# Two pads of 352 bytes per partition that move the feed-forward's later weight parts and the experts' second weights in on-chip memory

## The chip, the cores and the metric

The program runs on one core of a Trainium2 chip. The metric is the device time of one execution in microseconds (us). Before the change it is 1409.03 us, the median of three runs (1408.67, 1409.03 and 1420.4).

## What is computed

An attention with pooled keys and values, then a layer of eight experts of which each token uses at most one, then a dense feed-forward. The last part, cut to its core, is

```python
def _moe2_ref(x, w_in, w_out):       # x [4608, 512], w_in [512, 2048], w_out [2048, 512]
    h = x @ w_in
    g = h * (1.0 / (1.0 + np.exp(-h)))
    return (g @ w_out).astype(np.float32)
```

and inside the expert layer each expert computes `np.maximum(xc @ w1[e], 0.0) @ w2[e]`, with `w1[e]` of 512 x 1024 and `w2[e]` of 1024 x 512. Everything is float32 to the outside, and the feed-forward's weights come as float64 words that the kernel converts itself.

## The kernel before, in words

The three stages run one after the other: attention, experts, feed-forward. Matmuls of the experts and of the feed-forward use a reduced float32 format (F32R). To keep accuracy each operand is split in a high and a low half, and each product is made of three matmuls: high by high, high by low, low by high.

**Feed-forward.** The hidden dimension of 2048 is cut into 16 parts f = 0 to 15 of 128, the 4608 tokens into 9 blocks of 512 (block 8 first, then down to 0, as `ORDER` says). `ffn_load` brings part f of `w_in` and `w_out`, vector operations of `ffn_ops` turn the 64-bit words to float32, and `ffn_conv3` makes the halves: ScalarE casts `fh`, GpSimd subtracts to `fl`. Each is a tile of 4096 bytes per partition: 2048 bytes of `w_in`, then 2048 bytes of `w_out`. Parts 0 and 1 lie in a pool opened early, parts 2 and 3 in the room of the experts' first weights (`w1h`), and parts 4 to 15 in a pool `fwts` that is opened from the top end of the memory, after the experts are done. They stay there for all blocks.

A *visit* is one part f in one block. `mm1(b, f)` does 12 matmuls into the tile `fh<b>_<f>` in PSUM: the weights' 128 columns are loaded into the array (PEld in the profile), and the 512 rows of x^T, `fxh` and `fxl`, stream through it. These two lie in the room of `w1l`, and so the trace names them `w1l`. Sigmoid on ScalarE and a product on VectorE give g, which is split in `fgh` and `fgl`. `mm2(f - 1)` does 12 matmuls into `fop`: there 128 columns of `fgh` or `fgl` are loaded, and the 512 elements of `w_out`'s part stream. So the order on the matmul engine is mm1(0), mm1(1), mm2(0), mm1(2), mm2(1) and so on, with the transposes of the next block's x (`fxp`) at the end of a block. In all there are 9 x 16 x 24 = 3456 such matmuls, all of 512 columns; 9 x 12 x 24 = 2592 of them use parts 4 to 15.

The conversion of parts 3 to 15 is spread over the first visits: block 8 with parts 0 to 5, then block 7 with all 16, where the vector operations are put between those of the visits by the table `PACE`; then block 8 with parts 6 to 15. Every engine takes its instructions in program order.

The tile names of the profile: `fh`, `fl` are weight parts, but `fh<-...` in a matmul row is mm1's output tile; `w1h` as an input of `fh` or `fop` is part 2 or 3. The line of nearly every instruction is that of a helper (L111), so rows are told apart by their tiles.

**Experts.** `mm1` there streams the tokens `xth`, `xtl` (256, 320 or 384 columns, by how many tokens a unit has) against `w1h`, `w1l` into `hp`; `mm2` streams 512 elements of `w2h`, `w2l` against `hh`, `hl` into `yp`.

**Addresses.** Where each operand of these matmuls begins in its partition, by the built program, as the remainder of its byte address by 512. Slices inside a tile move it by multiples of 512 (`w_out`'s half by 2048, the 128-column slices by 512, the rows of x^T by 4096, the tokens' and hidden rows of the experts by 1536).

| operand | used in | address before | remainder before |
|---|---|---|---|
| `fxh`, `fxl` (in `w1l`) | mm1, streamed | 33408 | 128 |
| `fgh`, `fgl` (two buffers each) | mm2, loaded | 111232 to 117376 | 128 |
| parts 0, 1 | mm1 loaded, mm2 streamed | 74368 to 86656 | 128 |
| parts 2, 3 (in `w1h`) | the same | 17024 | 128 |
| parts 4 to 15 | the same | 131040 to 225248 | 480 |
| `w2h`, `w2l` | experts' mm2, streamed | 122528, 138912 | 160 |
| `hh`, `hl` | experts' mm2, loaded | 90752, 103040 | 128 |
| `xth`, `xtl` | experts' mm1, streamed | 201536, 207680 | 320 |
| `w1h`, `w1l` | experts' mm1, loaded | 17024, 33408 | 128 |

Of the kernel before, what the change touches and what calls it, by code (L numbers as in the profile page):

```python
# [5 lines left out]
F32 = mybir.dt.float32  # L6
# [12 lines left out]
P = 128  # L19
# [23 lines left out]
PACE = [3, 3, 3, 3] + [2, 3] * 8  # L43
HALF = 6
POOL = 8
ON0, ON1 = 3,0
OPS = [2, 2, 2, 0, 4, 4]
ORDER = list(range(NT // 512))[::-1]
# [7 lines left out]
def constants():  # L56
# [4 lines left out]
    c[:, C_IS:C_IS + SLOTS] = np.arange(SLOTS)[None, :]  # L61
    scale = 1.0 / (POOL * np.sqrt(D))
    c[:, C_E] = (p < D) * scale
    c[:, C_E + 1] = (p >= D) * scale
    for i, (h0, n) in enumerate(HEADS):
        for j in range(n):
            r = CP * i + p
            c[:, C_MV + HOFF[i] + j] = ((r // G == h0 + j) & (p < CP) & (r < H * G)) / POOL
    for t in range(9):
# [84 lines left out]
class Kern:  # L154
# [23 lines left out]
    def attention(self, xa, rs, extra):  # L178
# [3 lines left out]
        with tc.tile_pool(name="as", bufs=1) as s1, \  # L182
# [11 lines left out]
            def loadk(b):  # L194
                k_t[b] = s2.tile([P, 4, G, POOL], F32, name=f"k{b}", tag="k")
                nc.sync.dma_start(k_t[b].rearrange("p a g t -> p a (g t)"), self.kT[b])

            def loadv(b):
                v_t[b] = s2.tile([P, NC, POOL, D], F32, name=f"v{b}", tag="v")
                for c in (slice(0, ON0), slice(ON0, NC)) if b == 0 else (slice(NC),):  # L200
                    nc.sync.dma_start(v_t[b][:CP, c].rearrange("p c t d -> p c (t d)"), self.vR[b][:, c])
# [137 lines left out]
            nc.vector.memset(one, 0.0)  # L339
            k_t[0] = s2.tile([P, 4, G, POOL], F32, name="k0", tag="k")  # L340
            for a in (0, 2):
# [10 lines left out]
            for i in range(NB):  # L352
                nc.gpsimd.tensor_scalar(vex[i][:, :, D], mv, float(POOL), None, ALU.mult)
            for i in range(2):
# [413 lines left out]
    def moe_weights(self, pool):  # L768
        T = lambda n, shape: pool.tile(shape, F32R, name=n, tag=n)
        self.w2h, self.w2l = T("w2h", [P, 8, DM]), T("w2l", [P, 8, DM])  # L770

    def moe_first(self, pool, keep):
        T = lambda n, shape: pool.tile(shape, F32R, name=n, tag=n)
        self.w1h = keep.tile([P, 4, FM], F32R, name="w1h", tag="w1h")
        self.w1l = keep.tile([P, 4, FM], F32R, name="w1l", tag="w1l")
        self.fxh, self.fxl = self.w1l[:, :, 0:DM], self.w1l[:, :, DM:FM]
        self.raw1 = pool.tile([P, 4, FM], F32, name="raw1", tag="raw1")
        self.raw2 = pool.tile([P, 8, DM], F32, name="raw2", tag="raw2")
        self.xth, self.xtl = T("xth", [P, 4, U * P]), T("xtl", [P, 4, U * P])
        self.xn = pool.tile([P, U, XW], F32, name="xn", tag="xn")  # L780
        self.x4 = pool.tile([P, U + 1, XW], F32, name="x4", tag="x4")
        self.g0, self.gi, self.si = [pool.tile([P, U], I32, name=n, tag=n) for n in ("g0", "gi", "si")]
        self.sc = pool.tile([P, (U + 1) * E], F32, name="sc", tag="sc")
        self.m0 = pool.tile([P, E], F32, name="m0", tag="m0")
        self.mf = pool.tile([1, E], F32, name="mf", tag="mf")
        self.start = pool.tile([1, E], F32, name="start", tag="start")
        self.pick = pool.tile([1, 3, E], F32, name="pick", tag="pick")
        self.qv = pool.tile([1, 3], F32, name="qv", tag="qv")
        self.sel, self.nu = [pool.tile([1, 1], I32, name=n, tag=n) for n in ("sel", "nu")]
        self.qi = pool.tile([1, 2], I32, name="qi", tag="qi")  # L790
        self.sq = pool.tile([P, U], I32, name="sq", tag="sq")
        self.ut = pool.tile([1, 4, NU], I32, name="ut", tag="ut")
# [244 lines left out]
    def ffn_pool(self, pool):  # L1037
        self.fpool = pool
        self.fw = {}
        self.fraw = {}  # L1040

    def ffn_load(self, f, eng=None):
        eng = eng or self.nc.sync
        raw = self.fpool.tile([P, 2, DM], U64, name=f"fr{f}", tag=f"fr{f % 3}")
        eng.dma_start(raw[:, 0].rearrange("p (c n) -> p c n", c=4),
                          self.w_in[:, P * f:P * (f + 1)].rearrange("(c p) n -> p c n", p=P))
        eng.dma_start(raw[:, 1], self.w_out[P * f:P * (f + 1), :])
        w = raw.rearrange("p a n -> p (a n)").bitcast(U32).rearrange("p (n t) -> p n t", t=2)
        self.fraw[f] = w[:, :, 0], w[:, :, 1]
# [197 lines left out]
def build(tc, qT, kT, vR, wr, con, w1, w2, w_in, w_out, out):  # L1247
    k = Kern(tc, qT, kT, vR, wr, con, w1, w2, w_in, w_out, out)
    with tc.tile_pool(name="const", bufs=1) as cp, \
         tc.tile_pool(name="hp", bufs=3, space=PSUM) as k.hp, \  # L1250
         tc.tile_pool(name="dram", bufs=1, space=DRAM) as dr:
        xa = dr.tile([NT, XW], F32, name="xa", tag="xa")
        with tc.tile_pool(name="ab", bufs=1, side="right") as ab, \
             tc.tile_pool(name="ar", bufs=2, side="right") as ar, \
             tc.tile_pool(name="rp", bufs=1, space=PSUM) as rp:
            k.const_tiles(ab, cp)
            k.moe_first(ab, cp)
            k.rp = rp

            def expert0(i):  # L1260
                if i in (22, 27):
                    e0 = k.nc.value(k.sel[0:1, 0:1], E - 1, (mybir.EngineType.SP,))
                    (k.load_w1 if i == 22 else lambda e: k.load_w2(e, k.raw2))(e0)
                if 28 <= i < 32:
                    k.conv1(i - 28, k.nc.gpsimd)
                if i in (33, 34):
                    k.xtrans((2 * (i - 33), 2 * (i - 33) + 1))

            k.xa = xa
            k.attention(xa, ar, expert0)  # L1270
            with tc.tile_pool(name="mo", bufs=1, side="right") as mo:
                k.moe_weights(mo)
                fp = tc.alloc_tile_pool(name="fpre", bufs=1)
                k.ffn_pool(fp)
                with tc.tile_pool(name="un", bufs=1) as up:
                    k.moe(xa, up)
        with tc.tile_pool(name="fwts", bufs=1, side="right") as fw:
            k.ffn(xa, fw, dr)
        fp.release()


# [20 lines left out]
```

## Time and profile before

| | |
|---|---|
| median of 3 runs | 1409.03 us |
| the profiled execution | 1412.7 us, of which the span from first to last instruction is 1410.9 us |
| busy share of the span | matmuls (PE) 94%, weight loads (PEld) 79%, VectorE (DVE) 51%, ScalarE (ACT) 36%, GpSimd (POOL) 18% |
| attention and experts | 0 to about 573 us |
| feed-forward | about 573 us to the end |

Matmuls overlap each other in the records, so a busy PE does not say how fast it goes. The pace is read from the starts: the distance from one group of 12 matmuls to the next, divided by 12. The granted clock (PEclk) is 1.0 where TensorE runs at the higher of its two levels (2.4 GHz).

### The profile page before, as it was taken

How to read it: one execution, taken by the hardware profiler on the slowest of the kernel's cores; microseconds unless marked ns; L12 is line 12 of the kernel's file. 1: busy time of each engine (PE TensorE's matmuls, PEld its weight loads, DVE VectorE, ACT ScalarE, POOL GpSimd, SP SyncE). 2: the span in 40 equal slices, each digit the busy share in tenths (PEclk: the TensorE clock that was granted, in tenths of full speed). 3: DMA queues.
4: the chain of work that ended last, by engine and by line, in shares of the span. 5: the costliest groups of instructions: out<-in, count | busy, mean ns of one | idle time of the engine just before them, and what ended most of it. 6: DMA issues, size and time to landing. Idle time of an engine off the chain costs nothing.

```text
span 1410.9 us, 20283 instructions
## 1 busy us (share of the span) xinstructions
PE 1333.0 (94%) x6681; PEld 1115.0 (79%) x6682; DVE 717.1 (51%) x1380; ACT 508.1 (36%) x1093; POOL 260.5 (18%) x210
## 2 busy tenths in 40 slices
PE   5887889999899998889999999999999999999998
PEld 4776777888789887768778888888888888888887
DVE  4688898676776676769633223223232232322322
ACT  4545644454444544335422223222232232222322
POOL 4644453232342332313300000000000000000000
PEclk9989999999999999999999999999999999999999
DMA  9856746565565642334120101001010010100000
GB/s 280 266 163 218 253 157 224 170 211 179 175 209 193 200 159 82 134 109 161 60 90 18 43 0 60 0 1 60 1 60 0 1 60 0 48 13 1 30 1 30
DMA packets 58585, 145.39 MB, mean 103 GB/s; under 512 B 5855, under 2 KB 15455, under 8 KB 55882
## 3 DMA queue, kind: packets, MB, share of 16 engines
q1 hardware_dynamic: 52463, 127.79, 27.5%
q0 software_dynamic: 5760, 16.48, 3.4%
q8 instruction: 43, 0.70, 0.2%
q10 hardware_dynamic: 288, 0.19, 0.1%
q14 instruction: 31, 0.23, 0.0%
HBM read 117.47 MB, written 29.66 MB: 104 GB/s over the span
## 4 chain that ended last, share of the span: by engine, by line
PE 57%; DVE 2%; issue 1%; ACT 1%; POOLq 0%; POOL 0%; DVEq 0%; ACTq 0%
PE fh L111 27%; PE fop L111 27%; PE fxp L111 1%; PE yp L111 1%; PE hp L111 1%; DVE fr L111 1%; DVE ft L111 0%; ACT fsg L111 0%; DVE fgl L111 0%; DVE fsg L111 0%; POOLq L1298 0%; POOL fl L111 0%; DVE w2l L111 0%; ACT fgh L111 0%; ACT fm L111 0%
## 5 line engine op out<-in xcount | busy, mean ns | idle before, releaser
L111 DVE TENSOR_TENSOR fsg<-fh,fsg 128x512 f32<-128x512 f32 x144 | 99.5, 691 | 427.5 <-ACT fsg L111 427.5
L111 PE MATMUL fh<-w1l,fh 128*128 128x512 f32 x1008 | 255.5, 395 | 4.5 <-ACT fh L111 4.5
L111 ACT ACTIVATE fsg<-fh 128x512 f32<-128x512 f32 x144 | 86.2, 598 | 450.0 <-PE fh L111 450.0
L111 PEld LDWEIGHTS fh<-w1l,fh 128*128 128x128 f32 x1008 | 188.9, 188 | 51.1 <-ACT fh L111 6.2
L111 PE MATMUL fop<-fh,fgh 128*128 128x512 f32 x504 | 201.7, 400 | 0.0
L111 PE MATMUL fop<-fl,fgh 128*128 128x512 f32 x504 | 199.8, 396 | 0.0
L111 DVE TENSOR_TENSOR fgl<-fsg,fgh 128x512 fp32r<-128x512 f32 x144 | 99.5, 691 | 85.4 <-ACT fgh L111 85.1
L111 PE MATMUL fop<-fh,fgl 128*128 128x512 f32 x504 | 142.6, 395 | 0.2 <-DVE fgl L111 0.2
L111 PE MATMUL fh<-w1l,fl 128*128 128x512 f32 x504 | 138.1, 396 | 1.5 <-POOL fl L111 1.5
L111 ACT CAST fgh<-fsg 128x512 fp32r<-128x512 f32 x144 | 89.4, 621 | 119.8 <-DVE fsg L111 119.8
L111 PEld LDWEIGHTS fh<-w1l,fl 128*128 128x128 f32 x504 | 94.7, 189 | 25.2 <-POOL fl L111 3.3
L111 PEld LDWEIGHTS fop<-fh,fgl 128*128 128x128 f32 x504 | 94.8, 188 | 23.0 <-DVE fgl L111 0.7
L111 PEld LDWEIGHTS fop<-fh,fgh 128*128 128x128 f32 x504 | 95.0, 189 | 21.8 <-ACT fgh L111 0.2
L111 PEld LDWEIGHTS fop<-fl,fgh 128*128 128x128 f32 x504 | 95.1, 189 | 21.4
L111 PE MATMUL yp<-w2h,hh 128*128 128x512 f32 x240 | 96.8, 403 | 1.8 <-ACT w2h L111 1.4
L111 PE MATMUL yp<-w2h,hl 128*128 128x512 f32 x240 | 94.8, 395 | 0.0
L111 PE MATMUL yp<-w2l,hh 128*128 128x512 f32 x240 | 94.8, 395 | 0.0
L111 ACT ACTIVATE prb<-s,mx 128x72 f32<-128x72 f32 x288 | 65.0, 339 | 66.5 <-DVE mx L111 66.5
L111 ACT ACTIVATE hh<-hp 128x256 fp32r<-128x256 f32 (+2 forms) x96 | 41.2, 429 | 119.3 <-PE hp L111 112.3
L111 PE MATMUL hp<-xth,w1h 128*128 128x256 f32 (+2 forms) x384 | 71.3, 307 | 10.2 <-PEq L1298 6.5
L111 PE MATMUL hp<-xtl,w1h 128*128 128x256 f32 (+2 forms) x384 | 71.7, 306 | 3.7 <-DVE xtl L111 3.5
L111 PE MATMUL s<-kbd,q 128*128 128x144 f32 (+1 forms) x320 | 50.4, 313 | 21.3 <-ACT kbd L111 11.9
(190 smaller groups left out, 1984.6 us busy)
## 6 DMA issues: line engine op xcount, KB each, us to landing
raw<-w SPq DMA_DIRECT2D x96, 512.0 KB, 4.4
xa<-x SPq DMA_DIRECT2D x36, 260.0 KB, 3.6
fx<-xa SPq DMA_DIRECT2D x9, 1024.0 KB, 5.9
v<-vR SPq DMA_DIRECT2D x7, 1200.0 KB, 13.6
fr<-w_in SPq DMA_DIRECT2D x16, 512.0 KB, 4.0
fr<-w_out SPq DMA_DIRECT2D x16, 512.0 KB, 5.0
out<-fo SPq DMA_DIRECT2D x32, 256.0 KB, 2.4
k<-kT SPq DMA_DIRECT2D x7, 1152.0 KB, 9.0
```

The source lines that it names most:

```text
L111: ins = f(*a, **k)
```

## The change

Two pads, tiles of 352 bytes per partition that nothing reads, are allocated: one behind `w2l` in the pool of the experts' second weights, one behind part 15 in the feed-forward's pool. Both pools grow down from the top of the memory, so that all that lies before the pad in its pool begins 352 bytes lower.

```diff
+PAD = 352
 ...
     def moe_weights(self, pool):
         T = lambda n, shape: pool.tile(shape, F32R, name=n, tag=n)
         self.w2h, self.w2l = T("w2h", [P, 8, DM]), T("w2l", [P, 8, DM])
+        self.pad(pool, PAD, "pad_w2")
 ...
+    def pad(self, pool, n, name):
+
+        t = pool.tile([P, n // 4], F32, name=name, tag=name)
+        self.nc.gpsimd.memset(t[:, 0:1], 0.0)
 ...
         with tc.tile_pool(name="fwts", bufs=1, side="right") as fw:
             k.ffn(xa, fw, dr)
+            k.pad(fw, PAD, "pad_end")
```

By the built program these begin elsewhere, and nothing else does:

| operand | address now | remainder by 512 now (before) |
|---|---|---|
| parts 4 to 15 | 130688 to 224896 | 128 (480) |
| `w2h`, `w2l` | 122176, 138560 | 320 (160) |

On the matmul, vector, scalar and DMA queues every instruction and every wait stands where it stood. GpSimd gets two memsets of one column. The first comes in its queue behind the last one-hot operations of the token routing (`rm`, `rw`) and ahead of the first low halves of the experts' second weights (`w2l`). Before:

```order
92 L111 TENSOR_SCALAR rw_2350<-isb,sl_2341,consts 128x288
93 L111 TENSOR_SCALAR rm_2352<-iob,pf_2338 128x128 [waits PE_49]
94 L111 TENSOR_SCALAR rw_2354<-isb,sl_2341,consts 128x288
95 L111 TENSOR_TENSOR w2l<-raw_85,w2h 128x512 [waits DVE_49,DMAHW4_49,PE_49,DMAHW7_49,Activation_49,Pool_49]
96 L111 TENSOR_TENSOR w2l<-raw_85,w2h 128x512 [waits Activation_49]
```

And now:

```order
92 L112 TENSOR_SCALAR rw_2350<-isb,sl_2341,consts 128x288
93 L112 TENSOR_SCALAR rm_2352<-iob,pf_2338 128x128 [waits PE_49]
94 L112 TENSOR_SCALAR rw_2354<-isb,sl_2341,consts 128x288
95 L112 MEMSET pad_w_2411 128x1 [waits DVE_49,PE_49,DMAHW4_49,Activation_49,Pool_49]
96 L112 TENSOR_TENSOR w2l<-raw_85,w2h 128x512 [waits DMAHW7_49,Activation_49]
97 L112 TENSOR_TENSOR w2l<-raw_85,w2h 128x512 [waits Activation_49]
```

The memset has taken over most of the waits of the subtraction behind it, and none is new. The second memset is GpSimd's last instruction, behind the low half of part 15.

## Rows read from the trace of the kernel before

**Rows 1.** The page's chain that ended last: shares by engine.

```profile
PE 57%; DVE 2%; issue 1%; ACT 1%; POOLq 0%; POOL 0%; DVEq 0%; ACTq 0%
```

**Rows 2.** Busy time of each engine in stretches of the feed-forward, core 0.

```profile
core 0: us, PE busy (x) PEld busy (x) DVE busy (x) ACT busy (x) POOL busy (x), PEclk, DMA share, GB/s
...
631.00:701.00 70.00, 68.04 (x290) 54.07 (x290) 59.68 (x58) 31.14 (x40) 21.63 (x9) 1.00 0.36 121
...
875.00:966.00 91.00, 91.00 (x402) 73.89 (x402) 25.91 (x38) 22.89 (x39) 0.00 (x0) 1.00 0.07 24
```

**Rows 3.** Chain that ended last, block 5, parts 1 to 8: start, us, engine, tile, matmuls.

```profile
872.03 2.72 PE fh L111 x12
874.75 2.72 PE fop L111 x12
877.47 2.72 PE fh L111 x12
880.19 2.72 PE fop L111 x12
882.91 2.81 PE fh L111 x12
885.72 2.73 PE fop L111 x12
888.45 2.81 PE fh L111 x12
891.26 2.80 PE fop L111 x12
...
910.87 1.17 PE fh L111 x5
```

**Rows 4.** Timeline of PE at an expert's second product: start, us, out<-in, count.

```profile
469.68 0.39 PE L111 MATMUL yp<-w2h,hh 128*128 128x512 f32 x1
...
471.08 0.75 PE L111 MATMUL hp<-xth,w1h 128*128 128x320 f32 x4
```

**Rows 5.** The page's costliest groups: the experts' second product, one of three.

```profile
L111 PE MATMUL yp<-w2h,hl 128*128 128x512 f32 x240 | 94.8, 395 | 0.0
```

**Rows 6.** Timeline of PE at experts' first products of 384, 256 and 320 columns.

```profile
241.26 0.87 PE L111 MATMUL hp<-xth,w1h 128*128 128x384 f32 x4
...
244.09 0.87 PE L111 MATMUL hp<-xtl,w1h 128*128 128x384 f32 x4
...
390.02 0.62 PE L111 MATMUL hp<-xth,w1h 128*128 128x256 f32 x4
...
399.09 0.62 PE L111 MATMUL hp<-xth,w1l 128*128 128x256 f32 x4
...
414.80 0.74 PE L111 MATMUL hp<-xth,w1h 128*128 128x320 f32 x4
...
428.29 0.75 PE L111 MATMUL hp<-xth,w1l 128*128 128x320 f32 x4
```

**Rows 7.** PE's waits from 584 to 726 us: total, times, longest.

```profile
PE fh L111 <- ACT fh L111: 4.5, 4, 1.4
...
PE fh L111 <- POOL fl L111: 1.5, 4, 0.4
```

**Rows 8.** Timeline of block 7, all engines: part 14 becomes ready.

```profile
693.21 0.60 ACT L111 ACTIVATE fsg<-fh 128x512 f32<-128x512 f32 x1 [3.67 <-PE fh L111]
...
696.12 1.11 ACT L111 CAST fh<-fr 128x1024 fp32r<-128x1024 f32 x1
...
697.29 2.14 PE L111 MATMUL fh<-w1l,fh 128*128 128x512 f32 x8 [1.37 <-ACT fh L111]
```

**Rows 9.** Timeline of POOL where the first pad's memset comes in.

```profile
199.42 0.60 POOL L111 TENSOR_SCALAR rm<-iob,pf 128x128 f16<-128x128 f16 x1
...
201.30 1.28 POOL L111 TENSOR_TENSOR w2l<-raw,w2h 128x512 fp32r<-128x512 f32 x1
202.75 1.29 POOL L111 TENSOR_TENSOR w2l<-raw,w2h 128x512 fp32r<-128x512 f32 x1 [0.17 <-ACT w2h L111]
205.08 1.29 POOL L111 TENSOR_TENSOR w2l<-raw,w2h 128x512 fp32r<-128x512 f32 x1 [1.03 <-ACT w2h L111]
```

## The prediction

> **What bounds the kernel now.** I read the chain that ended last first. By its shares [rows 1] PE carries 57% of the span, and no other engine more than 2%. The stretches come next: in a steady block of the feed-forward PE is busy 91.00 of 91.00 us at a granted clock of 1.00, its higher level of 2.4 GHz, while VectorE is busy 25.91 and GpSimd not at all [rows 2]. So in the feed-forward the matmuls' own pace sets the time, and only what changes that pace counts.
>
> The third view gives the pace, and it is not the same everywhere. In block 5 the matmuls on parts 1 to 3 go in groups of 12 that take 2.72 us, and from part 4 on the groups take 2.81 and 2.80 us [rows 3], with the same shapes, the same clock and no wait. The group at 885.72, which starts behind part 4's mm1, is the second product of part 3 and takes 2.73 us: the step comes with the part that is used, not with the moment. From 872.03 to 882.91 two visits take 10.88 us, 5.44 each; from 888.45 to 910.87 four take 22.42 us, 5.605 each. That is 226.7 against 233.5 ns for a matmul. The table of addresses says what goes with it: for parts 0 to 3 both operands begin 128 bytes past a multiple of 512, for parts 4 to 15 the one at 128 and the other at 480. The slices of the loaded operand step by 512 through all the places of a part, and the pace of parts 1 to 3 does not follow them. So no larger unit than 512 seems to matter.
>
> **The change part by part.**
>
> *Feed-forward parts 4 to 15.* They now begin at 128 too. I take the row of parts 1 to 3 as their new pace: 5.605 - 5.44 = 0.165 us for a visit.
> - Blocks 6 to 0 have 12 such visits each, 84 in all: 84 x 0.165 = 13.9 us, all on the path, since PE waits for nothing there.
> - Block 8's second turn has 10 (parts 6 to 15): 1.65 us.
> - Block 7 has 12, worth 1.98 us, while conversion still runs. VectorE is busy 59.68 of 70 us there [rows 2], 85%; with visits 3% shorter that is 88%, so it doesn't become the bound. But PE waits for parts 14 and 15, on ScalarE's cast and then on GpSimd's subtraction [rows 7]. Part 14's cast ends a chain that begins when PE has done part 13's mm1 (693.21) and lets PE go at 697.29 [rows 8]; meanwhile PE has only the 12 matmuls of one mm2. Making those shorter by 12 x 6.8 ns = 0.08 us lengthens the wait by as much, and likewise the 8 matmuls ahead of the wait for the low half by 0.05. Twice, that gives back 0.27: 1.7 us remain (ends: 0 and 1.98).
> - Block 8's first turn has 2 (parts 4, 5), where PE waits for each conversion [rows 7]: 0 (ends: 0 and 0.33). The conversion hides them, and without that cover they would add to the gain.
>
> Together 13.9 + 1.65 + 1.7 = 17.2 us less.
>
> *Experts' second weights.* `w2h` and `w2l` go from 160 to 320, against `hh` and `hl` at 128. Now six matmuls take 471.08 - 469.68 = 1.40 us [rows 4], 233.3 ns each, like the feed-forward's later parts; there are three groups of 240 such matmuls [rows 5], 720 in all. No row has 320 with 128 at 512 columns, but the experts' first product has just these remainders at fewer columns [rows 6]: 384 columns take 2.83 us for four groups of four, 176.9 ns or 0.461 ns a column; 320 take 13.49 us for 23 groups, 146.6 ns or 0.458; 256 take 9.07 us for 20 groups, 113.4 ns or 0.443. At 512 columns 0.461 would be 235.9 ns, 2.6 more than now, +1.9 us over 720; 0.443 would be 226.7, the pace of the good parts, -4.8 us. The nearest sizes speak for the slow pace, so I take half the upper end: +1.0 us (ends: -4.8 and +1.9).
>
> *The pads' memsets.* GpSimd has no idle time at 201.30, so the first pad's memset delays the subtraction behind it. It has one column; the nearest row, 128 columns in 0.60 us [rows 9], bounds it from above, zero from below. The gaps that follow, 0.17 and 1.03 us of waiting for ScalarE [rows 9], take it up: 0. If they were gone, it would cost at most 0.6 us. The second stands behind all of GpSimd's work, which ends in block 7: 0.
>
> The sum is -17.2 + 1.0 = -16.2 us. On the profiled execution (1412.7 us, its span 1410.9) that gives 1396.5. That execution is 3.7 us above the median of 1409.03, so against the median I forecast **1392.8 us**, 1.15% less.
>
> **The rivals.**
>
> *It is the place, not the remainder.* All the fast parts lie below 91,000 bytes and all the slow ones above 131,000, and the change leaves that so. Then nothing changes and the time stays at 1409. For this speaks that no fast row lies high. Against it: the experts' `w2h` has its first four chunks below the mark of 131,072 and streams against `hh` at 90,752, yet its matmuls interleave with those of `w2l` above the mark at one pace of 233.3 ns [rows 4]. Also 384 columns from 201,536 and 320 columns cost as much a column as parts that begin elsewhere, and 256 columns from the same high place run at the fast rate [rows 6]. The Trainium skill bears on this rival: "TensorE: Matmul & The Clock Gate", Part 2, Step-by-step, says that weight loads and the streamed operand have two independent read ports, so that loading the next weights takes nothing from the running matmul; and "SBUF — State Buffer", Operand start alignment, asks for no more than a multiple of the element's size, as a rule of what is legal, without timings. By these pages where an operand begins would not matter. The steps of 2.72 and 2.81 us at one clock disagree with that. Chance 0.08.
>
> *Part of the gain only.* If just one of the two products gains (the loaded operand's place matters and not the streamed one's, or the other way round), half of 17.2 is left: 1409 - 8.6 + 1.0 = 1401.4. Against it: in rows 3 both `fh` and `fop` groups show the step. For it: parts 4 to 15 now begin 1024 off from parts 0 to 3 when counted by 2048, which no row has shown for a streamed weight. Chance 0.06.
>
> *The new remainders run slower.* Should parts 4 to 15 at their new places meet the pace of the worst row, 0.461 ns a column [rows 6], each of the 2592 matmuls would take 235.9 instead of 233.5 ns: +6.2 us, and the experts' +1.9, together 1417. It decides from any pace above 233.5 ns in the feed-forward. Against it stand the parts 1 to 3, which have this remainder on both sides and are the fastest rows of all. Chance 0.04.
>
> *A larger gain.* If 320 against 128 is good at 512 columns as it is at 256, the experts gain 4.8: 1409 - 17.2 - 4.8 = 1387. Chance 0.12.
>
> **How the numbers follow.** The forecast has the remaining 0.70. The three runs before agree within 0.4 us except one, and the profiled execution is 3.7 above the median, so I allow 2 to 3 us either way around the cases. The range of 8 in 10 then runs from 1386.0, just beyond the larger gain, to 1398.0, the forecast with block 7's gain lost (+1.7), the experts at +1.9 instead of +1.0 and that allowance. About 1% is what a measurement of this kernel can tell from no change; faster by more than that means under 1394.9. The larger gain and three quarters to four fifths of the forecast's cases lie there: 0.12 + 0.56 = 0.68. Within 1% are the rest of it, the unchanged and the halved case, and most of the slower one, which reaches only +0.6%: 0.30. Slower by over 1% would need some 240 ns for each of the 2592 matmuls: 0.02.
>
> **What the profile after would show.** The groups of 12 on parts 4 to 15 should take 2.72 us, and blocks 6 to 0 should each be 1.98 us shorter. If they still take 2.80, the place decides; if `fh` groups fall and `fop` groups don't, or the reverse, only one of the operands counts. In the experts six `yp` matmuls should take 1.40 to 1.42 us; 1.36 would be the larger gain. PE's waits for parts 14 and 15 in block 7 should be longer by some 0.3 us in all. What would make the forecast wrong without any of this: a change of the granted clock in the stretches where PE waits for conversions [rows 7].

## The result, and the profile after

The changed kernel takes 1395.88 us against 1410.22 of the kernel before (medians of four runs each); the ratio is 0.9872 with a 95% interval of 0.9822 to 0.9921. Timed again in six runs on another occasion it was 1393.21 against 1404.54 us, 0.9904 (0.9881 to 0.9926). One of the four runs of the changed kernel, 2186.86 us at a granted clock of 0.56, was disturbed and is left out of the ratio; the median of its other three is 1394.34 us, 15.9 less. The forecast was 1392.8 us, a ratio of 0.9885, in a range of 1386.0 to 1398.0.

The chain that ended last, in the same stretch of block 5 as [rows 3]: start, us, engine, tile, matmuls.

```profile
868.54 2.72 PE fh L112 x12
871.26 2.72 PE fop L112 x12
873.98 2.72 PE fh L112 x12
876.70 2.72 PE fop L112 x12
879.42 2.72 PE fh L112 x12
882.14 2.72 PE fop L112 x12
884.86 2.72 PE fh L112 x12
887.58 2.72 PE fop L112 x12
...
903.90 1.13 PE fop L112 x5
```

The step at part 4 is gone: every group of 12 takes 2.72 us, with part 4's first product at 879.42 and after it. Where [rows 3] had 2.81 and 2.80 there is now the pace of parts 0 to 3, at the same granted clock of 1.00.

A whole block is read from where the chain begins one block's last part and the next block's first (24 matmuls in a row). Of the kernel before:

```profile
863.84 5.47 PE fh L111 x24
954.67 5.47 PE fh L111 x24
```

And after:

```profile
860.38 5.44 PE fh L112 x24
949.25 5.44 PE fh L112 x24
```

90.83 us became 88.87, 1.96 less; the forecast said 1.98. By the starts of their first matmuls the stretches of the feed-forward compare so:

| stretch | before, us | after, us | difference | forecast |
|---|---|---|---|---|
| block 8, parts 0 to 5 | 47.28 | 47.66 | +0.38 | 0 |
| block 7 | 94.91 | 93.68 | -1.23 | -1.7 |
| block 8, parts 6 to 15 | 57.82 | 56.23 | -1.59 | -1.65 |
| blocks 6 to 1, each | 90.83 | 88.87 | -1.96 | -1.98 |
| block 0, to its last matmul | 88.85 | 86.81 | -2.04 | -1.98 |
| together, from the unrounded starts | | | -16.3 | -17.2 |

The experts' second product did not change its pace. The timeline of PE, to be read with [rows 4]: start, us, out<-in, count.

```profile
470.88 0.40 PE L112 MATMUL yp<-w2h,hl 128*128 128x512 f32 x1
471.12 0.39 PE L112 MATMUL yp<-w2h,hh 128*128 128x512 f32 x1
...
472.52 0.75 PE L112 MATMUL hp<-xth,w1h 128*128 128x320 f32 x4
```

From 471.12 to 472.52 are six matmuls and 1.40 us, as before. The pad's memset is there, on GpSimd:

```profile
200.86 0.12 POOL L112 MEMSET pad_w<- 128x1 f32 x1
200.92 2.71 POOL L112 TENSOR_TENSOR w2l<-raw,w2h 128x512 fp32r<-128x512 f32 x2
204.66 1.29 POOL L112 TENSOR_TENSOR w2l<-raw,w2h 128x512 fp32r<-128x512 f32 x1 [1.03 <-ACT w2h L112]
```

It takes 0.12 us, and the wait of 1.03 us for ScalarE behind it is the one of [rows 9]. It costs nothing. The second memset (0.10 us at 706.71) comes just ahead of part 15's low-half matmuls in block 7, whose wait was 0.39 us, 0.37 before.

Of the profiled executions, the span fell from 1410.9 to 1395.6 us, 15.3. The feed-forward gave 16.3 of it, and 1.0 was lost ahead of it. There the granted clock was lower, as the busy time of each engine in the first 560 us shows, with PEclk third from the end:

```profile
0.00:560.00 560.00, 497.36 (x3014) 441.14 (x3016) 403.29 (x972) 272.06 (x719) 216.96 (x193) 0.96 0.60 197
```

The kernel before had 0.97 there. The kernel with the experts' pad alone and the one with the feed-forward's pad alone (below) have 0.96 too, with feed-forwards of either kind, so I read no effect of the change in it.

### The profile page after: what moved, and what is told of

It reads as the page before. It is cut to its first block, busy times and chain, and to the rows that moved or that the text cites. A ratio compares the mean times of both kernels' runs of the same rounds, so it can differ in the third digit from the quotient of the medians.

```text
span 1395.6 us, 20285 instructions
## 1 busy us (share of the span) xinstructions
PE 1319.3 (95%) x6681; PEld 1117.7 (80%) x6682; DVE 714.2 (51%) x1380; ACT 508.0 (36%) x1093; POOL 259.4 (19%) x212
## 4 chain that ended last, share of the span: by engine, by line
PE 57%; DVE 2%; issue 1%; ACT 1%; POOL 0%; POOLq 0%; DVEq 0%; ACTq 0%
PE fh L112 27%; PE fop L112 26%; PE fxp L112 1%; PE yp L112 1%; PE hp L112 1%; DVE fr L112 1%; DVE ft L112 0%; ACT fsg L112 0%; POOL w1h L112 0%; DVE fgl L112 0%; DVE fsg L112 0%; POOLq L1306 0%; POOL fl L112 0%; DVE w2l L112 0%; ACT fgh L112 0%
## 5 line engine op out<-in xcount | busy, mean ns | idle before, releaser
L112 PE MATMUL fh<-w1l,fh 128*128 128x512 f32 x1008 | 249.7, 390 | 3.3 <-ACT fh L112 3.3
L112 PE MATMUL fop<-fl,fgh 128*128 128x512 f32 x504 | 196.7, 390 | 0.0
L112 PE MATMUL fh<-w1l,fl 128*128 128x512 f32 x504 | 135.3, 390 | 1.6 <-POOL fl L112 1.3
L112 PE MATMUL hp<-xth,w1l 128*128 128x256 f32 (+2 forms) x384 | 70.7, 306 | 0.0
## 6 DMA issues: line engine op xcount, KB each, us to landing
v<-vR SPq DMA_DIRECT2D x7, 1200.0 KB, 13.9
```

What stands on the lines that cost most here:

```text
L112: ins = f(*a, **k)
```

## The experiments

**One half of the change at a time.** The first kernel leaves out the experts' pad:

```diff
     def moe_weights(self, pool):
 ...
-        self.pad(pool, PAD, "pad_w2")
```

> Only the pad of the feed-forward's pool; the experts' second weights stay at 160. Theory (the feed-forward's parts carry the whole gain, 0.165 us a visit): matmuls on parts 4 to 15 at 226.7 ns, experts' yp at 233.3 ns, and the same time as the changed kernel within 1 us of its 1396, so 14 to 17 us under the kernel before. Rival (the moved second weights carry part of it): less than 12 us under the kernel before.

Measured: 1391.65 against 1408.81 us, ratio 0.9877 (0.9845 to 0.9909), 17.2 us less. Parts 4 to 15 go at 226.7 ns a matmul, `yp` at 233.3. The second kernel leaves out the other pad:

```diff
             k.ffn(xa, fw, dr)
-            k.pad(fw, PAD, "pad_end")
```

> Only the pad of the experts' second weights (320 instead of 160); parts 4 to 15 stay at 480. Theory: yp matmuls still 233.3 ns, parts 4 to 15 still 233.5 ns, no change against the kernel before (0 us, within 3). Rival (the second weights' move pays): yp at 226.7 ns and 4.8 us less.

Measured: 1407.94 against 1408.81 us, ratio 0.9991 (0.9967 to 1.0014). `yp` stays at 233.3 ns. So the feed-forward's pad carries the gain, and from moving the second weights from 160 to 320 no gain shows.

**Which remainders are good.** One kernel gives each later part a place of its own, 32 bytes on from the one before, with x and g at 128 (the experts' pad is left out here, and where the grain is looked for below):

```diff
+            if f > 4:
+                self.pad(pool, 32, f"pad{f}")
             h, l = [(pool or self.fpool).tile([P, 2, DM], F32R, ...
 ...
-            k.pad(fw, PAD, "pad_end")
```

> Each later part begins 32 bytes further than the one before: part 4 at 128, part 5 at 160, up to part 15 at 480; streamed x and loaded g stay at 128. One look at the pace of each part. Theory of equal remainders (both operands must begin at the same remainder by 512): only part 4 at 226.7 ns, all others slower, 230 to 236. Rival theory of a boundary (a multiple of 64 is enough): parts 4, 6, 8, 10, 12, 14 at 226.7 and parts 5, 7, 9, 11, 13, 15 at 233. Rival with a multiple of 128: parts 4, 8 and 12 at 226.7.

The chain in block 5 there, from part 4's first product (879.77) to part 5's second (893.53):

```profile
879.77 2.72 PE fh L112 x12
882.49 2.73 PE fop L112 x12
885.22 2.79 PE fh L112 x12
888.01 2.72 PE fop L112 x12
890.74 2.80 PE fh L112 x12
893.53 2.79 PE fop L112 x12
```

The `fh` group of part 4 (879.77) still takes 2.72 us, that of part 5, at 160, 2.79 (885.22). Over the steady blocks the mean distance from one matmul's start to the next inside a group, in ns, is (the second products of parts 14 and 15 without the distances that a transpose interrupts):

| part | 4 | 5 | 6 | 7 | 8 | 9 | 10 | 11 | 12 | 13 | 14 | 15 |
|---|---|---|---|---|---|---|---|---|---|---|---|---|
| remainder | 128 | 160 | 192 | 224 | 256 | 288 | 320 | 352 | 384 | 416 | 448 | 480 |
| mm1 (part loaded) | 226.6 | 232.9 | 233.6 | 233.3 | 233.2 | 232.9 | 229.9 | 233.4 | 228.5 | 232.6 | 233.6 | 233.3 |
| mm2 (part streamed) | 227.1 | 233.3 | 229.9 | 233.3 | 231.7 | 233.5 | 233.3 | 233.4 | 228.7 | 233.3 | 229.8 | 233.8 |

A boundary of 64 or 128 bytes is out: parts 6 and 8, at 192 and 256, are slow on the loaded side. Part 4 alone has the full pace as its mean, as equal remainders ask; 256 further on (384) comes nearest, at 228.5 and 228.7. On a part between, what it costs differs with the side on which it stands, and not all lie in the 230 to 236 that were expected (229.9 for parts 6 and 10 on one side).

The table holds more than the theory. Places that are 256 apart agree to 0.5 ns on either side (160 and 416, 192 and 448, 224 and 480), but for 128 and 384. In mm1 the pairs of 192 and 224 do so at each place in the group of 12, to 0.1 ns. And of part 12, at 384, only the first matmuls of a group are slow, as its second product in block 5 shows:

```profile
932.40 0.39 PE L112 MATMUL fop<-fh,fgh 128*128 128x512 f32 x1
...
933.55 0.39 PE L112 MATMUL fop<-fl,fgh 128*128 128x512 f32 x1
...
935.14 2.03 PE L112 MATMUL fh<-w1l,fh 128*128 128x512 f32 x8
```

The first five matmuls take 1.15 us, 230 ns each, the other seven 1.59 us, 227 each. So the table speaks for a unit of 256 rather than 512, which the three theories had not named; no kernel has all later parts at 384, where it would show. The time of this kernel, in its one run, was 1406.43 us.

**Equal, or 128?** All operands of the feed-forward go to 160, and `hh`, `hl` too, which the second weights then meet:

```diff
+            k.pad(cp, 32, "pad_left")
             k.moe_first(ab, cp)
 ...
-        self.pad(pool, PAD, "pad_w2")
 ...
-            k.pad(fw, PAD, "pad_end")
+            k.pad(fw, 320, "pad_end")
```

> Every operand of the feed-forward begins at 160: a pad of 32 bytes ahead of the experts' first weights moves x, g and parts 0 to 3 there, and a pad of 320 the parts 4 to 15; hh and hl move to 160 with them and meet the second weights, which stay at 160. Theory of equal remainders: all feed-forward matmuls at 226.7 ns, and the experts' yp at 226.7 instead of 233.3, so 17 + 4.8 = 22 us under the kernel before. Rival theory of a boundary (160 is no multiple of 64): all of them at 233.5 ns, parts 0 to 3 too, so 864 x 6.8 ns = 5.9 us over the kernel before.

Its chain in block 5, the first products of parts 4 and 5 and the second ones of parts 3 and 4:

```profile
874.88 2.72 PE fh L112 x12
877.60 2.72 PE fop L112 x12
880.32 2.72 PE fh L112 x12
883.04 2.72 PE fop L112 x12
```

And its timeline in the experts:

```profile
459.25 0.39 PE L112 MATMUL yp<-w2h,hh 128*128 128x512 f32 x1
...
461.74 0.39 PE L112 MATMUL yp<-w2h,hl 128*128 128x512 f32 x1
```

Every group of the feed-forward takes 2.72 us at 160, and 11 `yp` steps take 2.49 us, 226.4 ns each (over all of them a mean of 226.9 to 228.0, where it was 233.3 before). The number 128 has no part in it: what counts is that the two operands begin at the same remainder. The time was 1392.38 against 1408.81 us, ratio 0.9883 (0.9841 to 0.9924), 16.4 us less and not the 22 expected, which the interval just holds. Some of it may have gone to the experts' first product, which meets 320 with 160 here: its 256-column matmuls rose from a mean of 114.3 to 118.7 ns, 2.1 us over 480 of them.

**To the byte?** All later parts lie in one tile, at 0 to 96 bytes past 128:

```diff
+FINE = [0, 1, 2, 3, 4, 5, 6, 7, 8, 12, 16, 24]
 ...
+            if pool and not hasattr(self, "big"):
+                self.big = pool.tile([P, 24664], F32R, name="fhl", tag="fhl")
+            if pool:
+                a = 2048 * (f - 4) + FINE[f - 4]
+                h, l = [self.big[:, a + d:a + d + 1024].rearrange("p (a n) -> p a n", a=2) for d in (0, 1024)]
```

> The later parts in one tile that begins at 128, each a few bytes past it: part 4 by 0, parts 5 to 11 by 4, 8, 12, 16, 20, 24 and 28 bytes, parts 12 to 15 by 32, 48, 64 and 96; x and g stay at 128, the experts' second weights at 160. If the two remainders have to be equal to the byte: part 4 alone at 226.7 ns, all others 230 to 236. If a line of 16 bytes is the grain: parts 4 to 7 (0 to 12 bytes) at 226.7, the rest slower. If 32 or 64 bytes are: parts 4 to 11, or 4 to 13, at 226.7.

The chain in block 5, from part 4's first product (874.45) to part 7's first (891.03):

```profile
874.45 2.72 PE fh L113 x12
877.17 2.73 PE fop L113 x12
879.90 2.78 PE fh L113 x12
882.68 2.75 PE fop L113 x12
885.42 2.77 PE fh L113 x12
888.19 2.84 PE fop L113 x12
891.03 2.73 PE fh L113 x12
```

Part 4's matmuls take 226.7 ns in mm1 as a mean, part 5's, one element of 4 bytes further, 232.4 (the 2.78 at 879.90), and its mm2 236.4 (the 2.84 at 888.19). At 8 bytes it is 231.0 and 234.1, at 16 bytes 233.4 and 231.7. Two places come near the good pace: 12 bytes with 227.7 (the 2.73 at 891.03) and 229.0, and 28 bytes with 227.5 in mm2 but 233.6 in mm1. So no line of 16, 32 or 64 bytes is the grain, and one element is enough to lose the pace. But the strict theory fell too, which had part 4 alone at the good pace: at 12 bytes in mm1 only the first matmul of a group is slow (240 ns), and from the second on they take 225 to 227. And part 4's own second product, with equal remainders, took a mean of 229.0 here (2.75 at 882.68): its first five matmuls, behind a group of part 5, took 229 to 235 ns, the others 226 to 228. The one run took 1401.37 us.

**The experts too.** The second weights go to 128, where `hh` and `hl` are:

```diff
-        self.pad(pool, PAD, "pad_w2")
+        self.pad(pool, 32, "pad_w2")
```

> The change, with the experts' second weights at 128 (a pad of 32 instead of 352 behind them), like hh and hl. Theory of equal remainders: yp at 226.7 to 228 ns instead of 233.3, 720 times, so 4 to 4.8 us under the kernel with only the feed-forward's pad, some 21 us under the kernel before, as far as PE is what the experts' stage waits for. Rival (the experts' stage hides it: conversions and gathers set its length): yp faster, but the first feed-forward matmul no earlier and the time within 2 us of the kernel with only the feed-forward's pad.

Measured: 1388.57 against 1408.12 us, ratio 0.9871 (0.984 to 0.9901), with `yp` at 227.1 to 228.0 ns. From the end of one such product in the repeated run (below):

```profile
461.86 0.39 PE L112 MATMUL yp<-w2h,hl 128*128 128x512 f32 x1
...
464.12 0.75 PE L112 MATMUL hp<-xth,w1h 128*128 128x320 f32 x4
```

Ten matmuls take 2.26 us, 226 ns each. The next kernel adds a pad that brings the experts' x to 128 as well (with the change's own pads, all operands then stand there):

```diff
             k.rp = rp
+            k.pad(ab, 192, "pad_x")
```

> The same and the experts' x at 128 too (a pad of 192 behind it in its pool), like w1h and w1l: all operands of experts and feed-forward at 128. Theory of equal remainders: yp at 226.7 to 228 ns, hp at 170 ns for 384 columns (176 before), 141.7 for 320 (146.6) and 113.3 for 256: 288 x 6 + 384 x 5 = 3.6 us more than with the second weights alone, 25 us under the kernel before. Rival (the stage hides it): the paces fall, the time stays within 2 us of the kernel with only the feed-forward's pad.

Measured: 1389.63 against 1408.12 us, ratio 0.9862 (0.9831 to 0.9893), no better by its median. The first product did not do what was expected:

```profile
383.98 0.64 PE L112 MATMUL hp<-xth,w1h 128*128 128x256 f32 x4
...
393.57 0.64 PE L112 MATMUL hp<-xth,w1l 128*128 128x256 f32 x4
...
408.26 0.74 PE L112 MATMUL hp<-xth,w1h 128*128 128x320 f32 x4
...
421.75 0.75 PE L112 MATMUL hp<-xth,w1l 128*128 128x320 f32 x4
```

With 256 columns 20 groups of four take 9.59 us, 119.9 ns a matmul and more than the 113.4 of [rows 6]. With 320 columns it is 146.6 ns, as before. With 384 columns the median fell from 176 to 173 ns. But the kernel with all of the feed-forward at 160, where 320 meets 160, has 173 as well, and the changed kernel in its first profile 174, with the addresses of before. So equal remainders are shown as a rule for 512 columns, not for fewer. The half of the theory that promised a gain there fell.

**The change and the better version on one chip.** The change as it is:

> The changed kernel once more, for a narrower interval. By the paces (2592 matmuls at 226.7 instead of 233.5 ns, less what conversion gives back) 16 to 17.5 us under the kernel before, a ratio of 0.988; if the attention's and the experts' clock windows shift with it, up to 3 us off that.

Measured: 1393.21 against 1404.54 us, ratio 0.9904 (0.9881 to 0.9926). The gain of 11.3 us is less than the 16 expected, though its feed-forward, 817.2 us from the first to the last matmul (before 833.9), is as short as in the first run; the experts' stage ahead of it, from its first matmul to the feed-forward's first, took 382.0 us in this profile and 377.0 in the first. The version with the second weights at 128:

> The change with the experts' second weights at 128 once more, on the same chip as the change itself. Equal remainders pay there too: 4 us (720 matmuls by 5.7 ns) under the change. Rival (the experts' stage hides it): within 2 us of the change.

Measured: 1388.9 us, ratio 0.9882 (0.9864 to 0.99). It is 4.3 us under the change by the medians, as 720 matmuls by 5.7 ns give, and both times it had the lowest median of its series. The two intervals overlap a little, so the times alone don't settle it. The pace of `yp` shows that the matmuls gained, and the length of the experts' stage speaks for its reaching the time: 373.0 to 375.5 us in the four profiles with the fast `yp` (374.2 as a mean), 375.6 to 382.0 in the seven others (378.6).

## Why the prediction was right, point by point

*What bounds the kernel* held. The matmuls' pace set the feed-forward, and the pace moved the time.

*The pace of parts 1 to 3 as the new pace* held to the digit: 2.72 us a group. That is the step on which the forecast stood, and it was read from the kernel before, which had good and bad pairs side by side. The argument that no larger unit than 512 matters held too: parts 4 to 15 now stand 1024 off from parts 0 to 3 when counted by 2048, and run alike.

*Blocks 6 to 0 and block 8's second turn* gave 13.8 us and 1.59 where 13.9 and 1.65 were forecast.

*Block 7* gave 1.23, not 1.7. The waits for parts 14 and 15 grew as the prediction said: on the cast of part 14 from 1.37 to 1.49, on its subtraction from 0.36 to 0.41. With part 15's (0.33 to 0.40, and 0.37 to 0.39) that is 0.26 us, where 0.27 was forecast.

```profile
697.45 2.11 PE L112 MATMUL fh<-w1l,fh 128*128 128x512 f32 x8 [1.49 <-ACT fh L112]
...
699.97 0.74 PE L112 MATMUL fh<-w1l,fl 128*128 128x512 f32 x2 [0.41 <-POOL fl L112]
```

Most of the rest is at block 7's first part, from whose first matmul to the next part's it took 2.91 instead of 2.74 us, since its first matmul (386 ns) still ran at the lower clock, and at part 5, with 5.59 instead of 5.62 where 5.46 was due: there the weight load of part 4's second product (649.42) now waits 0.28 us for ScalarE's cast of g, a wait that the prediction did not have. The first matmul takes 339 ns instead of 234, and the five behind it 229 to 235.

```profile
649.42 0.19 PEld L112 LDWEIGHTS fop<-fh,fgh 128*128 128x128 f32 x1 [0.28 <-ACT fgh L112]
```

*Block 8's first turn* was 0.38 longer. The busy times from 584 to 631 us, with PEclk third from the end, are of before

```profile
584.00:631.00 47.00, 39.24 (x160) 30.02 (x159) 28.43 (x32) 18.75 (x26) 9.73 (x4) 0.93 0.32 113
```

and of after

```profile
584.00:631.00 47.00, 40.09 (x158) 30.53 (x157) 27.93 (x32) 18.22 (x25) 8.21 (x4) 0.89 0.32 113
```

The granted clock fell from 0.93 to 0.89 where PE waits for conversion. That is how the forecast said it could miss, and it was small. It isn't shown to be an effect of the change: the repeated run of the changed kernel has 0.93 there and 47.38 us for the turn, and the kernel with only the experts' pad, whose feed-forward is that of before, 1.00 and 45.43.

*The experts* were forecast at +1.0 and gave 0: `yp` is at 233.3 ns before and after. The term was small, but the reading behind it was wrong. I took the experts' first product at 384 and 320 columns as a measure of what 320 against 128 costs. The kernel with all operands at 128 shows that the paces at fewer columns don't follow the remainders as 512 columns do. That 320 against 128 is slow at 512 columns was right by luck.

*The pads' memsets* cost nothing, as said: 0.12 us under a wait.

*The rivals.* Place instead of remainder is out: the later parts lie where they lay, 352 bytes lower, and run at 226.7 ns. The rule that the Trainium skill ("TensorE: Matmul & The Clock Gate", Part 2, Step-by-step) gives, that loading the next weights takes nothing from the running matmul, is not what this pair shows at 512 columns: a loaded operand moved by 4 bytes made 12 matmuls take 2.78 instead of 2.72 us. By what way the load's address comes to count, no run shows. "Only one product gains" is out, since both gained. "Slower" and "a larger gain" would each have needed another pace than 226.7 or 233.3, and neither is there.

*The sum.* 16.3 us in the feed-forward against 17.2 forecast, and 15.3 in the whole span. The medians gave 14.3 or 15.9, and 11.3. Over the profiles, the seven feed-forwards whose operands all begin alike took 817.0 to 817.8 us from their first to their last matmul, but for one with 814.8, while the time ahead of it went from 562 to 574 us over all profiles. So what the median shows of a gain of 16 us moves by some us from series to series.

What stays open is the mechanism. The runs show that the pace depends on how the start addresses of the two operands stand to each other, on the number of columns, and for some matmuls on what ran just before. They don't show what in the chip the two reads share, nor why 256 columns ran slower with equal remainders.

## What to carry to other kernels

Where matmuls of 512 float32 columns run without waits, look at their pace by operand, not only at their busy share. Here a step of 3% at one clock and one shape came from addresses, and a pad of a few hundred bytes removed it. The safe choice by these runs is that the two operands of a matmul (the one loaded, the one streamed) begin at the same remainder by 512, to the element; 128 and 160 did equally well. It is not the only good one, as 256 bytes apart came within 1% of it. For fewer columns this does not carry over: read the pace there before moving anything.

## What was not expected of the hardware

- With equal remainders the pace is not only better, it is also the same everywhere: 226 to 227 ns for nearly all matmuls, at 128 and at 160. Behind a wait it takes a few matmuls to settle: in part 4's second product in block 7, after the wait of 0.28 us, the changed kernel shows 231, 235, 229, 232 and 231 ns, and then 227. With unequal ones it is mostly between 228 and 240 and depends on the position in the group of 12.
- One element matters: 4 bytes cost 5.7 ns in mm1 and 9.7 in mm2, about as much as the larger offsets. Yet 12 bytes in mm1 cost only 1.0.
- At 256 columns equal remainders are the worse case: 119.9 ns against 113.4 in [rows 6], with x at 320 and weights at 128.
- At unequal remainders the pace of 256 columns differs between kernels with the same addresses of these operands: a mean of 114.3 ns in the kernel before, 117.0 with the second weights at 128. The matmuls have two paces there, 113 to 114 and 116 to 119 ns, and their shares differ: 369 and 98 of 472 in the kernel before, 83 and 388 of 472 with the second weights at 128.
